# Joint steps for the first layer's sets 1 to 3, and the second layer's operands made from the sums

## The chip, the cores and the metric

The kernel runs on one core of a Trainium2 chip. The metric is device microseconds of one execution, the median of three runs. Lower is better.

## The reference

Attention with a forgetting decay, followed by two feed-forward layers, all in float32:

```python
scores = scale * q @ k.T ; scores = where(causal, -1e9, scores + decay)
x = softmax(scores) @ v                   # (4*576 tokens, 8*64 columns) = (2304, 512)
h = x @ w_in   ; x = (h - tanh(h)) @ w_out           # w_in (512, 2048), w_out (2048, 512)
h = x @ w_in2  ; x = (h * sigmoid(h)) @ w_out2       # the result
```

The weights arrive as float64; the kernel decodes them on the chip from their two 32-bit halves.

## The kernel before

**Numbers in two parts.** Each float32 matrix is split into a high part that TensorE takes without loss and a low remainder. A product is then three matmuls: high by high, high by low, low by high. The high part is a cast on ScalarE (ACT), the low part a subtraction on VectorE (DVE).

**Units.** The two layers are worked in 24 units: layer `l` (2), set `s` of 512 hidden columns (4, that is two weight chunks `q` of 256), token block `b` of 768 tokens (3). Units 0 to 11 are layer 1, units 12 to 23 layer 2. A product of two matrices cut 2 by 2 takes eight block products in the plain way; with sums and differences of blocks (Strassen's scheme) it takes seven. The seven operands of the token side are made once in a layer, written to DRAM (`xd`), and loaded again in each later unit.

**Slots.** Units below `U0` = 15 go through `slot_steps`, two slots a unit. A slot takes seven block products for `w_in` (`product`, L457; the first two units take eight, `plain`, L471). Each product lands in a PSUM bank, and DVE adds the products up one by one (L510). `bend` (L484) applies tanh or silu on ACT and, in layer 1, subtracts on DVE (L489). `high` and `low` split the result, and `project` (L427) takes eight block products for `w_out`, 96 matmuls of 384 columns a unit in layer 1; `gather` (L447) adds the sums to `x`. The operands of layer 2 are made in units 12 to 14 by `xtemp` (L324) and `xmake` (L337, L338, L342), a part of them on GpSimd (POOL).

**Joint steps.** Units 15 to 23 go through `joint`. There `h_step` (L634) and `c_step` (L675) take seven steps each for `w_in` and `w_out`, 12 or 18 matmuls a step, and add the products up inside PSUM. Between the steps ACT copies one running sum over another (L804, L870), so that fewer DVE additions are left. The steps of one unit's `w_out` alternate on TensorE with the next unit's `w_in`: h, c, h, c. `gate` (L797) applies the function, four times a unit; `two` (L807) makes the sums of the results, L839 and L840 split them, `gain` (L878) adds to `x`.

**What sets the order.** Every engine works through a fixed list. In the slots the list is written out by hand. In `joint` each piece of work is a `task` with an engine, a cost and a time at which it is meant to run, in steps of 2,080 ns; `planned` (L923) plays the list through and sorts it. TensorE's tasks keep their order; DVE and ACT take what is ready, at most three steps ahead of its time. The `keen` ones go first. The plan has no entry for a DMA.

**Weights.** `wjob` decodes a chunk: a scaling on ACT (L198), then shift, exponent, low, join on DVE (L202, L206, L209, L221), four sums of 256 columns (L225), and a split (L234 and L236 in the slots, L243 and L245 in `joint`). In the slots `w_out` needs no sums. There is one raw buffer for each of the two matrices; the load of the next chunk is issued after `low` (L160).

Of the kernel before, what the change touches and what calls it, by code (L numbers as in the profile page):

```python
# [37 lines left out]
U0 = 15  # L38
S0 = U0 // 3

# [4 lines left out]
def forgetting_attention_two_ffn(  # L45
# [106 lines left out]
    def wload(q, m, parts=(0, 1)):  # L152
# [17 lines left out]
        (((0, 4, 2),), ((8, 2, 6), (10, 1, 1))),  # L170
# [19 lines left out]
    def wjob(q, m, what, part=None):  # L190

        st = wjobs.setdefault((q, m), {})
        l, blocks = 2 * q // NFC, m == 0 or q >= 2 * S0
# [43 lines left out]
        else:  # L237
            for to, n, frm in GROUPS[m and l + 1][part]:
                hi, lo = (extra if to >= 8 else wtile)(q, m)
                to %= 8  # L240
                hi, lo, frm = hi[:, to:to + n], lo[:, to:to + n], st["s"][:, frm:frm + n]
# [350 lines left out]
    def ftile(u, what):  # L592
        k = u % 2
        if what == "12":
            if "12" not in small_tiles:
                small_tiles["12"] = pools["xb"].tile([P, 2, 2, TH], F32, tag="xo7", name="f_12")
            return small_tiles["12"][:, k]
        if what == "21":
            return flat(f"21_{k}", "hp", f"h{k}")
        if what == "1":  # L600
            return flat("1", "tp", "t0")
        if what == "22":
            return flat("22", "tp", "t1")
        return flat(what, "xt", {"a": "xt1", "b": "xt2"}[what])
# [4 lines left out]
    def ring_load(n):  # L609
# [4 lines left out]
        pool, tag = RING[n % 3]  # L614
        ring[u, i] = t = pools[pool].tile([P, 2, 2, TH], F32R, tag=tag, name=f"xr{n}")
        nc.sync.dma_start(out=rd(t).rearrange("p r k t -> p (r k t)"), in_=xd[l, b, i])
# [38 lines left out]
    def csteps(u):  # L655
        return STEPS if u < LASTU else (1, 5, 6, 2, 7, 3, 4)

    def c_step(u, k):
        l, i = units[u][0], csteps(u)[k]
        acc, fresh = cbank(u, i)  # L660
        t = gtile(7 * u + k)
        at = WAT[l][i]
        ws = [[w[:, at % 8] for w in (extra if at >= 8 else wtile)(2 * (u // NB) + j, 1)] for j in range(2)]
        for d in range(3 if l else 2):
            ds = slice(d * P, d * P + P)
            for j, (wh, wl) in enumerate(ws):
# [7 lines left out]
                for r, (w, m) in enumerate(terms):  # L674
# [3 lines left out]
                    )  # L678

# [24 lines left out]
    def joint():  # L704
        tasks, steps = [], 14
        tt_, copy = nc.vector.tensor_tensor, nc.scalar.copy

        def task(when, eng, cost, fn, reads=(), writes=(), keen=False):
            tasks.append((when, eng, cost, fn, reads, writes, keen))
# [7 lines left out]
        W2, N2 = dve(TB), act(TB)  # L717
        base = {u: steps * (u - U0) for u in range(U0, len(units) + 1)}
# [3 lines left out]


        def decode(q, m, when):
            l = 2 * q // NFC
            st = wjobs.setdefault((q, m), {})
            job, raw = (lambda *a: lambda: wjob(q, m, *a)), ("raw", m)

            def low():
                fill((q, m, "low"))  # L730

            yield "A", act(DM * 2), job("scale"), (raw,), (raw,)
            yield "V", 0.33, job("shift"), (raw,), ("wa",)
            yield "V", 0.33, job("exponent"), ("wa",), ("wb",)
            yield "V", dve(1024), low, (raw,), ("wb", raw)
            yield "V", dve(1024), job("join"), ("wa", "wb"), tuple(("ws", k) for k in range(4))
            for k, (to, p, op, r) in enumerate(RECIPE[m and l]):
                yield "V", dve(256), job("sum", k), (("ws", p), ("ws", r)), (("ws", to),)
            for g in range(2):
                cols = [("ws", k) for to, n, f in GROUPS[m and l + 1][g] for k in range(f, f + n)]  # L740
                n = 256 * len(cols)
                yield "A", act(n), job("HI", g), cols, (wkey(q, m, g),)
                yield "V", dve(n), job("LO", g), cols + [wkey(q, m, g)], (wkey(q, m, g),)

        def spread(t0, t1, parts):

            parts = [p if isinstance(p[0], float) or isinstance(p[0], int) else (None,) + p for p in parts]
            total = sum(c for _, e, c, *_ in parts if e == "V")
            t = t0
            for at, e, c, fn, r, w in parts:  # L750
                if at is not None:
                    t = max(t, at)
                task(t, e, c, fn, r, w)
                if e == "V":
                    t += (t1 - t0) * c / total

        for g in range(S0, 2 * NSET):
            t = base[3 * g]
            e, o = 2 * g + 2, 2 * g + 3
            if g == S0:  # L760
                a, b = list(decode(e - 2, 1, 0)), list(decode(o - 2, 1, 0))
                at = [(t + 2, a[-2]), (t + 10.5, b[-4]), (t + 14, b[-2])]
                parts = a + b
                t0, t1 = t, t + 16
            else:
                a, b = list(decode(o - 2, 0, 0))[-2:], list(decode(o - 2, 1, 0))
                at = [(t + 8.5, b[-4]), (t + 14.5, b[-2])]
                parts = a + b
                t0, t1 = t - 1, t + 15
            spread(t0, t1, [((next((w for w, p in at if p is j)),) if any(p is j for _, p in at) else ()) + j for j in parts])  # L770
            if e < 2 * NPR:
                a, b, c = list(decode(e, 0, 0)), list(decode(e, 1, 0)), list(decode(o, 0, 0))[:-2]
                at = t + 36.2
                parts = a + b + c
                spread(t + 16, t + 40, [((at,) if j is c[-2] else ()) + j for j in parts])


        for u in range(U0, len(units) + 1):
            t0 = base[u]
            if u < len(units):  # L780
# [13 lines left out]
                def gate(when, to, frm, kt, kf, tmp=None):  # L794
# [21 lines left out]
                gate(t0 + 11.55, g22, g22, f22, f22)  # L816
                gate(t0 + 12.0, g12, g12, f12, f12)
                if l:
# [8 lines left out]
                two(t0 + 15.3, g21, g21, tb, MINUS, f21, f21, fb, False)  # L827
# [5 lines left out]
                when[1], when[2] = 14.0, 14.5  # L833
                if u == LASTU:
                    when = dict(enumerate((10, 13.3, 13.4, 14.6, 15.6, 16.6, 17.6)))
                for k, i in enumerate(order):
                    n = 7 * u + k
                    g, (frm, kf), kg = gtile(n), src[i], n % 3
                    task(t0 + when[k], "A", N2, lambda g=g, f=frm: copy(g[:, 0], f), (kf,), (("gh", kg),))  # L839
                    task(t0 + when[k] + 0.1, "V", W2, lambda g=g, f=frm: tt_(g[:, 1], f, rd(g[:, 0]), MINUS),  # L840
                         (kf, ("gh", kg)), (("gl", kg),))
            v = u - 1
            if v < U0:
                task(t0 + 0.1, "A", 0, lambda: rest())
                for k in range(-1, 7):
# [561 lines left out]
```

## Time and profile before

| | before |
|---|---|
| median of three runs | 923.53 us (923.47 to 923.53) |
| the profiled execution's own time | 923.4 us |
| its span, first to last instruction | 921.4 us |
| TensorE busy, matmuls | 911.8 us (99%), 6006 |
| DVE busy | 764.8 us (83%) |
| ACT busy | 505.2 us (55%) |
| POOL busy | 174.0 us (19%) |
| granted TensorE clock, mean | 0.999 |

The profile is of one execution. Its span is 2.0 us shorter than that execution's time. Attention fills about the first 165 us; the slots run from there to about 634 us and the joint steps from 634 us to the end. A busy matmul is pipelined: its listed duration overlaps that of the next one, so the cost of one is read from start to start. The same holds, to a lesser degree, for DVE.

### The profile page before, as it was taken

What the parts mean: (1) busy time and instruction counts of PE and PEld (TensorE: products, weight loads), DVE (VectorE), ACT (ScalarE), POOL (GpSimd) and SP (SyncE); (2) the same over time, 40 slices, a digit from 0 to 9 for tenths busy, and PEclk for the clock granted to TensorE, in tenths of its full rate; (3) what the DMA queues carried; (4) which work ended last, traced back from release to release, by engine and by line L of the source; (5) the groups of instructions that cost most, each with busy time, mean ns of one, the idle gap of its engine ahead of it and who ended that gap; (6) DMA issues with size and microseconds to landing.
All of it is one profiled execution on the core that took longest, in us unless ns stands there. A gap on an engine that the chain in (4) does not pass through costs nothing.

```text
span 921.4 us, 15985 instructions
## 1 busy us (share of the span) xinstructions
PE 911.8 (99%) x6006; PEld 857.4 (93%) x6006; DVE 764.8 (83%) x1326; ACT 505.2 (55%) x871; POOL 174.0 (19%) x248
## 2 busy tenths in 40 slices
PE   8999999999999999999999999999999999999997
PEld 6777777799999999999999999899899999999997
DVE  7799998889878887888789898886779988977647
ACT  6888888666444332324242445564666666655443
POOL 8999999300000000000000010110000000000000
PEclk9999999999999999999999999999999999999999
DMA  5424442567548554855585456565677657655653
GB/s 166 150 97 159 160 139 84 220 249 298 222 199 331 208 206 158 331 180 220 172 304 190 169 206 217 186 232 210 244 247 255 233 199 269 200 178 200 210 184 121
DMA packets 48125, 188.94 MB, mean 205 GB/s; under 512 B 9456, under 2 KB 14064, under 8 KB 48016
## 3 DMA queue, kind: packets, MB, share of 16 engines
q1 hardware_dynamic: 47768, 187.64, 57.3%
q8 instruction: 47, 0.77, 0.3%
q10 hardware_dynamic: 280, 0.28, 0.1%
q14 instruction: 30, 0.25, 0.1%
HBM read 148.44 MB, written 38.34 MB: 203 GB/s over the span
## 4 chain that ended last, share of the span: by engine, by line
PE 95%; DVE 2%; ACT 1%; issue 1%; POOL 0%; DMA 0%; DVEq 0%; POOLq 0%
PE a L427 26%; PE h L457 20%; PE a L675 14%; PE h L634 14%; PE t L1139 5%; PE s L1092 5%; PE out_t L1195 4%; PE h L471 3%; PE s L1084 2%; PE h L675 0%; PE out L1195 0%; PE out_t L1223 0%; ACT gh L496 0%; POOL p L1127 0%; DMA de<-x 0%
## 5 line engine op out<-in xcount | busy, mean ns | idle before, releaser
L457 PE MATMUL h<-xo,wh 128*128 128x384 f32 x728 | 185.0, 334 | 0.0
L457 PEld LDWEIGHTS h<-xo,wh 128*128 128x128 f32 x728 | 132.0, 188 | 2.6
L634 PE MATMUL h<-xr,wh 128*128 128x384 f32 x504 | 128.5, 335 | 0.3 <-ACT h L804 0.3
L427 PE MATMUL a<-gh,wh 128*128 128x384 f32 x384 | 128.4, 334 | 0.0
L427 PE MATMUL a<-gl,wh 128*128 128x384 f32 x384 | 128.3, 334 | 0.0
L427 PE MATMUL a<-gh,wl 128*128 128x384 f32 x384 | 128.3, 334 | 0.0
L487 ACT ACTIVATE t<-hs 128x768 f32<-128x768 f32 x52 | 44.0, 847 | 145.9 <-DVE hs L510 145.9
L510 DVE TENSOR_TENSOR hs<-h,hs 128x384 f32<-128x384 f32 x182 | 100.6, 553 | 26.7 <-PE h L457 23.8
L457 PE MATMUL h<-xo,wl 128*128 128x384 f32 x364 | 121.8, 335 | 0.0
L634 PEld LDWEIGHTS h<-xr,wh 128*128 128x128 f32 x504 | 88.5, 189 | 1.4 <-ACT h L804 0.7
L338 POOL TENSOR_TENSOR xo<-xt,xo 128x768 fp32r<-128x768 f32 x3 | 6.2, 2071 | 425.8 <-ACT xo L337 425.8
L634 PE MATMUL h<-xr,wl 128*128 128x384 f32 x252 | 84.4, 335 | 0.0
L675 PE MATMUL a<-wh,gr 128*128 128x256 f32 x420 | 80.7, 282 | 0.0
L1113 ACT ACTIVATE p<-p,mn 128x128 f32<-128x128 f32 (+3 forms) x128 | 71.2, 558 | 16.9 <-DVE mn L1105 14.2
L1127 POOL TENSOR_SCALAR p<-p,sm 128x128 f32<-128x128 f32 (+3 forms) x128 | 72.7, 584 | 7.4 <-DVE sm L1124 6.9
L427 PEld LDWEIGHTS a<-gh,wh 128*128 128x128 f32 x384 | 72.1, 188 | 0.3 <-DVE x L447 0.3
L427 PEld LDWEIGHTS a<-gl,wh 128*128 128x128 f32 x384 | 72.1, 188 | 0.0
L427 PEld LDWEIGHTS a<-gh,wl 128*128 128x128 f32 x384 | 72.1, 188 | 0.0
L1105 DVE CUSTOM_DVE_ANT_0 p<-s,mask 128x128 f32<-128x128 f32 (+3 forms) x128 | 59.6, 479 | 14.3 <-PE s L1092 14.2
L500 DVE TENSOR_TENSOR gl<-t,gh 128x768 fp32r<-128x768 f32 x60 | 57.1, 952 | 14.1 <-ACT gh L496 13.9
L496 ACT CAST gh<-t 128x768 fp32r<-128x768 f32 x60 | 50.3, 839 | 32.8 <-DVE t L489 27.9
L457 PEld LDWEIGHTS h<-xo,wl 128*128 128x128 f32 x364 | 68.3, 188 | 0.0
(143 smaller groups left out, 2084.6 us busy)
## 6 DMA issues: line engine op xcount, KB each, us to landing
xo<-xd SPq DMA_DIRECT2D x63, 768.0 KB
xr<-xd SPq DMA_DIRECT2D x63, 768.0 KB
xd<-xo SPq DMA_DIRECT2D x42, 768.0 KB
raw<-w_in SPq DMA_DIRECT2D x32, 512.0 KB
raw<-w_out SPq DMA_DIRECT2D x32, 512.0 KB
kqraw<-kq SPq DMA_DIRECT2D x16, 608.0 KB
vraw<-v SPq DMA_DIRECT2D x16, 320.0 KB
out<-x SPq DMA_DIRECT2D x11, 384.0 KB
```

The costliest lines, as they stand in the source:

```text
L427: nc.tensor.matmul(dst, w, m, start=first and r == 0, stop=last and r == 2)
L457: nc.tensor.matmul(dst, w[:, ks], m[:, k], start=k == 0 and r == 0, stop=k == 1 and r == 2)
L496: nc.scalar.copy(gh, hs[h])
L500: nc.vector.tensor_tensor(gl, hs[h], rd(gh), ALU.subtract)
L510: nc.vector.tensor_tensor(to, p, s, ALU.add)
L634: nc.tensor.matmul(dst[:, j, 0:TH], w[:, ds], m[:, d], start=i in (1, 5) and d == r == 0, stop=d == 1 and r == 2, skip_group_check=True,)
L675: nc.tensor.matmul(dst, w, m, start=fresh and (l == 0 or d != 1) and j == r == 0, stop=j == 1 and r == 2, skip_group_check=True,)
L1092: nc.tensor.matmul(s[:, h, c:c + n], a[half(h), q], b[half(h), 0:n], start=r == 0, stop=r == 3,)
L1105: nc.vector.tensor_tensor_reduce(out=pt.rearrange("p (g c) -> p g c", g=2) if i == 4 else pt, in0=src, in1=m, op0=ALU.add, op1=ALU.min, sc ...
L1113: nc.scalar.activation(pt, pt, AF.Exp, bias=mn, scale=-1.0, accum_out=sums[:, n // 3 % 5, n % 3, 0:1],)
L1127: nc.gpsimd.tensor_scalar(pt, pt, sm[:, j:j + 1], 1.0, ALU.mult, ALU.mult)
L1139: nc.tensor.transpose(t[:, k], pt[:, c * P:c * P + P], ident)
```

## The change

`U0` goes from 15 to 3: units 3 to 14 leave the slots and enter `joint`. Units 3 to 11 (layer 1, sets 1 to 3) take seven steps for `w_in` and seven for `w_out`. Units 12 to 14 (layer 2, set 0), named `PLAIN`, take seven steps for `w_in` and eight block products for `w_out` (`plain_c`), whose sums ACT copies to `x`.

The operands of layer 2 are made by tasks in `joint` (`make`): four sums on DVE for each token block, in place in `x` (one of them in a spare tile, `tmp`), then seven splits (a cast on ACT, a subtraction on DVE) into the ring of three operand tiles from which `h_step` reads. Each is then written to DRAM by a DMA on SyncE's queue (`spill`). In the slots before, two of each unit's subtractions stood on POOL. The ring is loaded from DRAM for all other units.

In layer 1 a gate is a tanh on ACT and a subtraction on DVE; two of the four write the tanh to `tmp`. `planned` may now take a task up to eight steps ahead of its time (`EARLY`), and picks by a due time, the planned time plus a `spare`. Units 12 to 14 are planned one step longer. What was left of unit 2's work (`rest` and the first two of its remaining `project` calls) is issued ahead of the plan. The chunks of set 4 (layer 2, set 0) need no sums for `w_out`.

```diff
-U0 = 15
+U0 = 3
 S0 = U0 // 3
+PLAIN = (12, 13, 14)
+PLAINSETS = {u // NB for u in PLAIN if u >= NB * NSET}
...
-        l, blocks = 2 * q // NFC, m == 0 or q >= 2 * S0
+        l, blocks = 2 * q // NFC, m == 0 or q >= 2 * S0 and q // 2 not in PLAINSETS
...
+    def spill(n):
+        u, i = U0 + n // 7, STEPS[n % 7]
+        l, s, b = units[u]
+        d = xd[l, b, i] = dram.tile([P, 4 * TH], F32, name=f"xd{l}_{b}_{i}")
+        nc.sync.dma_start(out=d, in_=rd(ring[u, i]).rearrange("p r k t -> p (r k t)"))
...
+    def plain_c(u, c, a, t):
+        l, s, b = units[u]
+        acc, i = csums(u)[a], c // 10 - 1
+        fresh, last = i == 0 and s == 0, i == 1
+        for d in range(2 - a if l else 2):
+            for j in range(2):
+                q = 2 * (u // NB) + j
+                gh, gl = (t[:, e, j] for e in range(2))
+                if l:
+                    ds = slice((2 * a + d) * P, (2 * a + d) * P + P)
+                    wh, wl = (w[:, 2 * i:2 * i + 2].rearrange("p k f -> p (k f)") for w in wtile(q, 1))
+                    dst, terms = acc[:, d], ((gh[:, ds], wh), (gh[:, ds], wl), (gl[:, ds], wh))
...
     def joint():
-        tasks, steps = [], 14
+        rest()
+        for n in range(2):
+            project(16 * (U0 - 1) + n, False)
+        tasks = []
...
+            base[u + 1] = base[u] + 14 + (u - 1 in PLAIN)
...
+            if g == S0:
+                late = list(decode(o - 1, 1)) + late
+                spread(t, t + 15, late, at(o - 1, 1, 1, t + 2) | at(o, 1, 0, t + 10.5) | at(o, 1, 1, t + 11))
...
+        def make(u):
+            b, t0 = units[u][2], base[u]
...
+            def total(when, to, p, r, op=MINUS):
+                task(t0 + when, "V", W2, lambda: tt_(q[to](), q[p](), q[r](), op), (key[p], key[r]), (key[to],), False, 2)
+            total(-3.9, "11", "12", "11")
+            if less:
+                total(-3.5, "12", "22", "12", PLUS)
+                total(-1.5, "t", "12", "11")
...
+            total(0, "21", "21", "t")
...
+                kr, when = ("xr", n % 3), t0 + 2 * k - 4.6
+                def low(n=n, f=f):
+                    t = ring_tile(n)
+                    tt_(t[:, 1], q[f](), rd(t[:, 0]), MINUS)
+                    spill(n)
+                task(when, "A", N2, lambda n=n, f=f: copy(ring_tile(n)[:, 0], q[f]()), (key[f],), (kr,), False, 2)
+                task(when + 0.1, "V", W2, low, (key[f], kr), (kr,), False, 2)
...
-                    r = [kd] + [wkey(q + j, 0, k // 4) for j in range(2)]
+                    r = [kd, ("xr", (7 * (u - U0) + k) % 3)] + [wkey(q + j, 0, k // 4) for j in range(2)]
...
-                    t, k = (tmp, "tmp") if tmp is not None else (to, kt)
-                    task(when, "A", N2, lambda f=func: nc.scalar.activation(t, frm, f), (kf,), (k,), True)
-                    task(when + 0.45, "V", W2, lambda: tt_(to, frm, t, MINUS), (kf, k), (kt,), True)
+                    t, k = (lambda: ftile(0, "tmp"), "tmp") if tmp else (lambda: to, kt)
+                    task(when, "A", N2, lambda f=func: nc.scalar.activation(t(), frm, f), (kf,), (k,), True)
+                    task(when + 0.45, "V", W2, lambda: tt_(to, frm, t(), MINUS), (kf, k), (kt,), True)
...
-        LAG = 0.1
+        LAG, EARLY = 0.1, 8
...
-                return max([end[d] + LAG * (tasks[d][1] != e) for d in deps[n]] + [tasks[n][0] - 3])
+                return max([end[d] + LAG * (tasks[d][1] != e) for d in deps[n]] + [tasks[n][0] - EARLY])
```

## Rows read from the trace of the kernel before

**Rows 1.** The page's first part: busy us (share of the span), instructions.

```profile
PE 911.8 (99%) x6006; PEld 857.4 (93%) x6006; DVE 764.8 (83%) x1326; ACT 505.2 (55%) x871; POOL 174.0 (19%) x248
```

**Rows 2.** Busy us of each engine in stretches of the span.

```profile
core 0: us, PE busy (x) PEld busy (x) DVE busy (x) ACT busy (x) POOL busy (x), PEclk, DMA share, GB/s
240.00:500.00 260.00, 260.00 (x1502) 260.00 (x1501) 216.58 (x302) 97.18 (x121) 0.00 (x0) 1.00 0.61 225
630.00:680.00 50.00, 49.69 (x282) 46.16 (x281) 37.83 (x49) 30.02 (x38) 0.00 (x0) 1.00 0.64 223
680.00:710.00 30.00, 30.00 (x214) 29.73 (x213) 28.83 (x36) 19.55 (x25) 0.00 (x0) 1.00 0.65 221
770.00:800.00 30.00, 30.00 (x214) 29.91 (x214) 29.21 (x38) 18.29 (x23) 0.00 (x0) 1.00 0.65 221
680.00:800.00 120.00, 120.00 (x851) 119.45 (x850) 108.21 (x138) 74.47 (x94) 0.00 (x0) 1.00 0.68 230
```

**Rows 3.** Timeline of TensorE, joint steps: start us, us, then the instruction.

```profile
713.75 0.28 PE L675 MATMUL a<-weh,gr 128*128 128x256 f32 x1
713.87 0.28 PE L675 MATMUL a<-wel,gr 128*128 128x256 f32 x1
...
715.18 0.34 PE L634 MATMUL h<-xr,wl 128*128 128x384 f32 x1
715.35 0.51 PE L634 MATMUL h<-xr,wh 128*128 128x384 f32 x2
```

**Rows 4.** Timeline of DVE in the joint steps, back to back.

```profile
700.40 0.95 DVE L886 TENSOR_TENSOR x<-x 128x768 f32<-128x768 f32 x1
701.27 0.95 DVE L840 TENSOR_TENSOR gr<-f,gr 128x768 fp32r<-128x768 f32 x1
702.14 1.22 DVE L245 TENSOR_TENSOR wl<-ws,wh 128x1024 fp32r<-128x1024 f32 x1
703.28 0.95 DVE L878 TENSOR_TENSOR x<-a,x 128x768 f32<-128x768 f32 x1
...
706.60 0.70 DVE L206 TENSOR_SCALAR wb<-wa 128x1024 uint32<-128x1024 uint32 x1
707.33 1.22 DVE L209 SCALAR_TENSOR_TENSOR wb<-raw,wb 128x1024 f32<-128x1024 uint32 x1
...
710.59 0.42 DVE L225 TENSOR_TENSOR ws<-ws 128x256 f32<-128x256 f32 x1
710.93 0.95 DVE L878 TENSOR_TENSOR x<-a,x 128x768 f32<-128x768 f32 x1
...
720.50 0.68 DVE L202 TENSOR_SCALAR wa<-raw 128x1024 uint32<-128x1024 uint32 x1
721.10 0.95 DVE L807 TENSOR_TENSOR f_a<-f,f 128x768 f32<-128x768 f32 x1
```

**Rows 5.** DVE timeline, then TensorE timeline: one split, and the step that reads it.

```profile
696.33 0.95 DVE L840 TENSOR_TENSOR gr<-f,gr 128x768 fp32r<-128x768 f32 x1
...
699.98 0.28 PE L675 MATMUL a<-wh,gr 128*128 128x256 f32 x1
```

**Rows 6.** Timelines of SyncE's queue and of ACT, start of the joint steps.

```profile
640.24 0.81 SPq L160 DMA_DIRECT2D raw<-w_out  x2
...
645.05 1.14 ACT L198 ACTIVATE raw<-raw 128x1024 f32<-128x1024 f32 x1
```

**Rows 7.** POOL's groups from 500 to 660 us: busy us, mean ns.

```profile
L338 POOL TENSOR_TENSOR xo<-x,xo 128x768 fp32r<-128x768 f32 x3 | 6.7, 2236 | 0.0
L338 POOL TENSOR_TENSOR xo<-xt,xo 128x768 fp32r<-128x768 f32 x3 | 6.2, 2071 | 425.8 <-ACT xo L337 425.8
```

**Rows 8.** Waits of SyncE's queue: total us, times, longest us.

```profile
SPq L342 <- DVE xo L338: 115.9, 29, 14.7
```

More of the change, by code (lines that the diff above doesn't have):

```diff
@@ L715, in act, with decode @@
             return (n / 0.96 + 60) / 2080
-        W2, N2 = dve(TB), act(TB)
-        base = {u: steps * (u - U0) for u in range(U0, len(units) + 1)}
+        W2, N2, basis = dve(TB), act(TB), {}
+        base = {U0: 0}
+        for u in range(U0, len(units)):
+            base[u + 1] = base[u] + 14 + (u - 1 in PLAIN)
         def wkey(q, m, k):
             return "w", q % NSLOT, m, k
-        def decode(q, m, when):
+        def decode(q, m):
             l = 2 * q // NFC
[L726 to L736, printed above, removed]
-            for k, (to, p, op, r) in enumerate(RECIPE[m and l]):
[L738 to L743, printed above, removed]
@@ L745, in spread @@
-        def spread(t0, t1, parts):
-            parts = [p if isinstance(p[0], float) or isinstance(p[0], int) else (None,) + p for p in parts]
-            total = sum(c for _, e, c, *_ in parts if e == "V")
+            job, raw = (lambda *a: lambda: fill((q, m) + a)), ("raw", m)
+            yield "A", act(DM * 2), job("scale"), (raw,), (raw,), None
+            yield "V", 0.33, job("shift"), (raw,), ("wa",), None
+            yield "V", 0.33, job("exponent"), ("wa",), ("wb",), None
+            yield "V", dve(1024), job("low"), (raw,), ("wb", raw), None
@@ new lines, in decode @@
+            if m and q // 2 in PLAINSETS:
+                key = wkey(q, 1, 0)
+                yield "V", dve(1024), job("join"), ("wa", "wb"), ("wa",), None
+                yield "A", act(1024), job("hi"), ("wa",), (key,), 0
+                yield "V", dve(1024), job("lo"), ("wa", key), (key,), None
+                return
+            yield "V", dve(1024), job("join"), ("wa", "wb"), tuple(("ws", k) for k in range(8)), None
+            for k, (to, p, op, r) in enumerate(RECIPE[m and l]):
+                yield "V", dve(256), job("sum", k), (("ws", p), ("ws", r)), (("ws", to),), None
@@ new lines, in decode, with spread @@
+            groups = [0, 1, 2] if m and q // 2 in MIXED else [0, 1]
+            for g in groups[::-1] if m and q % 2 and 3 * (q // 2) - 1 in PLAIN else groups:
+                cols, key = [("ws", k) for to, n, f in GROUPS[m and l + 1][g] for k in range(f, f + n)], wkey(q, m, g)
+                yield "A", act(256 * len(cols)), job("HI", g), cols, (key,), g
+                yield "V", dve(256 * len(cols)), job("LO", g), cols + [key], (key,), None
+        def spread(t0, t1, jobs, since):
+            total = sum(c for e, c, *_ in jobs if e == "V")
@@ L759, in joint @@
-            e, o = 2 * g + 2, 2 * g + 3
+            t, t2 = base[3 * g], base[3 * g + 3]
+            o = 2 * g + 1
+            late = list(decode(o, 1))
             if g == S0:
[L761 to L764, printed above, removed]
-            else:
[L766 to L775, printed above, removed]
+                late = list(decode(o - 1, 1)) + late
+                spread(t, t + 15, late, at(o - 1, 1, 1, t + 2) | at(o, 1, 0, t + 10.5) | at(o, 1, 1, t + 11))
+            elif 3 * g - 1 in PLAIN:
+                spread(t - 1, t + 15, list(decode(o, 0))[-2:] + late, at(o, 1, 0, t + 15))
+            else:
+                spread(t - 1, t + 15, list(decode(o, 0))[-2:] + late, at(o, 1, 0, t + 8.5) | at(o, 1, 1, t + 14.5))
@@ L923, in planned @@
     def planned(tasks):
-        LAG = 0.1
+        LAG, EARLY = 0.1, 8
         tasks = sorted(tasks, key=lambda t: t[0])
         writer, readers, deps = {}, {}, []
-        for n, (when, eng, cost, fn, reads, writes, keen) in enumerate(tasks):
+        for n, (when, eng, cost, fn, reads, writes, keen, due) in enumerate(tasks):
             d = {writer[k] for k in reads if k in writer}
@@ L955, in planned @@
                 now = [n for r, n in known if r <= t]
-                n = min(now, key=lambda n: tasks[n][0])
-                if not tasks[n][6] and tasks[n][0] > t - 2:
+                n = min(now, key=lambda n: tasks[n][7])
+                if not tasks[n][6] and tasks[n][7] > t - 2:
                     soon = [r for r, k in known if tasks[k][6] and t < r < t + tasks[n][2] - 0.2]
```

147 lines of the change are left out of this document (115 added, 32 removed).

## The prediction

> **What bounds the kernel now.** I read the page's first part, then the stretches, then single instructions in the timelines. TensorE is busy for 99% of the span and DVE for 83% [rows 1]. A busy share alone proves little for an engine that pipelines, so the stretches come next. In layer 1's slots, 240 to 500 us, TensorE is busy for all of 260 us with 1502 matmuls of 384 columns [rows 2]: 260 / 1502 = 0.173 us from one to the next. The joint steps, 680 to 800 us, show no idle time either, and their matmuls follow each other at 0.17 us for 384 columns and 0.12 us for 256 [rows 3]. So TensorE sets the time; what is taken from it comes off the end, as long as no other engine takes its place. The next in line is DVE: 108.21 of 120 us in the joint steps [rows 2]. ACT, with 74.47 of 120 us there, is far off.
>
> **What is removed.** A unit of layer 1 has 84 matmuls for `w_in` and 96 for `w_out` in the slots, and 84 and 84 in joint steps. Nine units (3 to 11) lose 12 each: 108 matmuls, each 0.173 us, **18.7 us**. A unit goes from 180 x 0.173 = 31.1 us to 168 x 0.173 = 29.1 us. Units 12 to 14 gain nothing: eight block products before and after, 72 matmuls of 512 columns each. So the page should count 6006 - 108 = 5898. The floor is 923.4 (the profiled execution's own time) - 18.7 = 904.7 us; the median of the runs lies 0.1 us above that execution, so 904.8 us.
>
> One rule bears on the size of this term. The Trainium skill ("TensorE: Matmul & The Clock Gate", section "Wait — 56ns, not 53.3ns?") gives back-to-back matmuls N / 2.4 GHz plus about 2.5 ns, an estimate of 162.5 ns for 384 columns and 17.6 us for 108 of them. The trace has 173 ns for these float32 matmuls, and the measurement decides; the sum keeps 18.7 us.
>
> **What is added on DVE in layer 1.** This is where the gain can go. I count a joint unit of layer 1 in instructions of 768 columns: two sums of the running products, four tanh subtractions (layer 2 has none, its gates are ACT's alone), four sums of the results, seven low parts, five additions to `x`: 22, against 18 for a joint unit of layer 2. Back to back one takes 0.87 us from start to start (700.40, 701.27, 702.14) [rows 4]. Over the nine units that is 9 x 22 = 198, plus three changes of basis, plus six instructions of `make` that are planned before unit 12 begins, less twelve that end behind that point (low parts, last sums and additions of unit 11, of which some replace unit 2's): 195 x 0.87 = 170 us. A weight chunk takes 0.60 + 0.73 + 1.14 + 1.14 + 4 x 0.34 + 1.14 + 0.60 + 0.34 = 7.05 us: shift, exponent, low, join, four sums, split [rows 4]; the split's part of 512 columns has no row there and is put at the shift's 0.60, a choice. Eleven whole chunks fall into the nine units, one without sums (4.7 us) and one nearly whole (6.1 us): 88 us. Together **258 us** of DVE, beside 9 x 29.1 = 262 us of TensorE: 98%.
>
> So the bound of the cost runs from 0 to this: in the joint steps of layer 2 DVE shows as busy for 108.21 / 120 x 29.6 = 26.7 us a unit (84 matmuls at 0.173 and 126 at 0.12 make a unit of 29.6 us); four more at their listed 0.95 us give 30.5 us a unit, 1.4 us above TensorE, 12.6 us over nine units. The listed durations overlap when DVE is packed, so I hold to the count. How full can DVE be while TensorE does not wait? The two densest stretches of 30 us have it at 28.83 and 29.21 us, 96 and 97%, with TensorE at 30.00 [rows 2]. 258 us packed at 97% need 266 us, 4 us over 262. The third set is worst: the chunks of set 4 and `make` come on top there. I take **5 us** of waiting on TensorE, between 0 and 12.6 us.
>
> **The chain behind the gate.** In layer 1 a gate's result is later by one DVE subtraction, 0.87 us. The tightest place is the second `c_step` of a unit. In layer 2 its low part ended at 697.28 us and the step began at 699.98 us, 2.7 us later [rows 5]. With the subtraction 1.8 us are left, so alone it costs nothing; with a filled queue on DVE it is part of the 5 us. Behind a late low part stand all of TensorE's steps.
>
> **The move of layer 2's operands.** `make` issues 11 instructions of 0.87 us on DVE for each of units 12 to 14, 21 in all of them the low parts. Before, 6 of these 21 stood on POOL at over 2 us each [rows 7]; so DVE has some 6 x 0.87 = 5 us more. Cover: those units need no products added on DVE, no combined results and no additions to `x` (ACT copies); 17 instructions and some 8 us of weights make 23 us beside a unit of 31 us. Without that cover the price would be the 5 us. The 21 writes to DRAM move from the slots into SyncE's queue of the plan; the count and bytes are the same. In that queue a write waits for DVE's low part, up to 14.7 us before [rows 8], and behind it stand the weight loads, planned many steps ahead, while the ring's own loads are not needed there. Nothing is added for it. The first `h_step` of layer 2 now waits for an operand that DVE has just made; its data are a unit old, and it is late only if DVE is. This is in the 5 us.
>
> **Looser order.** With eight steps instead of three, ACT's scaling of a chunk can be placed right behind the freeing of the raw buffer, and the plan knows nothing of the load between. The nearest row: load issued at 640.24 us, scaling begun at 645.05 us [rows 6], so at most 4.8 us. The worst place is unit 3, where two `w_out` chunks follow each other. ACT would stand still for up to 4.8 us, with 1 to 3 us of room before the next copy of a sum: 0 to 3 us once. I take 0, since the third step there has its slack, and keep 3 in the range. The seam of slots and joint steps cost 0.31 us at 630 to 680 us [rows 2]; it moves to unit 2 and keeps its price. In the last nine units the looser order can gain nothing, TensorE being full, and DVE's idle tenth covers a loss.
>
> **Sum.** 923.4 - 18.7 + 5 = 909.7 us, and 0.1 for the median: **909.8 us**.
>
> **Rivals.**
> *DVE keeps up.* The free tasks fill every gap and unit 3, which has less of `x` to add, takes work ahead. For it: 97% is already reached without a wait. Against: 98% would have to hold for nine units. 904.8 us, within 904.5 and 906.5. Chance 0.22.
> *DVE is the new bound.* The busy share, not the count, is right: 904.8 + 12.6 = 917.4 us; 915.5 to 921.7. Against: the overlap of listed durations in rows 4. Chance 0.16.
> *Slower: the gate's chain in every unit.* DVE's list is fixed, and 1.8 us are left before the second `c_step`. If five other instructions (4.35 us) stand ahead of the low part, TensorE waits 2.5 us in each of nine units, 22.7 us, and the time is 904.8 + 22.7 = 927.5 us. It decides at 1.8 + 2.07 = 3.9 us of work ahead, four or five instructions, since a unit saves 2.07 us. For it: DVE is nearly full. Against: the gates are keen and go first. Chance 0.07.
> *The change doesn't do what it says.* If the nine units still issue 96 matmuls for `w_out`, the time stays at 923.5 us. The diff shows seven steps of 12; chance 0.05.
>
> **How the numbers follow.** The forecast, 906.5 to 915.5 us, has 0.50. The range of 904.5 to 920 us leaves out the slower case, the unchanged one and the upper end of the bound by DVE, some 0.15, and a little below. A measurement of this kernel can tell about 0.2%, 1.8 us: faster, below 921.7 us, 0.50 + 0.22 + 0.15 = 0.87; within, 0.06; slower 0.07.
>
> **What would show it.** 5898 matmuls; nine units of 29 to 30 us where 31.1 stood; DVE above 95% busy between units 3 and 12, and TensorE's idle time there some 5 us, ended by DVE or by ACT behind DVE, most of it near the end of layer 1; POOL idle after attention. Wrong would be: TensorE's gaps ended by a copy on ACT behind a scaling (the looser order), by an operand or weight load (SyncE's queue), or by DVE in every unit.

## The result, and the profile after

The changed kernel takes 930.09 us (median; 927.47 to 930.49) against 923.52 us before: a ratio of 1.0065, with a 95% interval of 1.0047 to 1.0084. It is slower by 6.6 us where 909.8 us was forecast, and it lies above the range of 904.5 to 920 us.

| | before | after |
|---|---|---|
| the profiled execution's own time | 923.4 us | 930.35 us |
| its span | 921.4 us | 927.7 us |
| matmuls | 6006 | 5898 |
| DVE busy | 764.8 us | 785.2 us |
| granted TensorE clock, mean | 0.999 | 0.993 |

The page's first part for the kernel after, as in [rows 1]:

```profile
PE 902.3 (97%) x5898; PEld 844.6 (91%) x5898; DVE 785.2 (85%) x1307; ACT 575.6 (62%) x969; POOL 161.2 (17%) x242
```

The 108 matmuls are gone, and TensorE's busy share still fell from 99% to 97%. Busy time of a pipelined engine says little about how much it waited, so I worked that out from the starts: the time from each matmul's start to the next one's, less the usual one (0.1735 us for 384 columns, 0.12 for 256, 0.23 for 512, as the kernel before has them), summed from 185 us on. Call it TensorE's lost time. It was 1.5 us before and is 26.7 us after. So -18.7 + 25.2 = +6.5 us, nearly the whole of the 6.95 us between the two profiled executions. The gain was made in full, and more than given back.

The stretches show where (columns as in [rows 2]; kernel after):

```profile
240.00:280.00 40.00, 35.12 (x193) 34.48 (x192) 31.18 (x44) 18.76 (x24) 0.00 (x0) 0.96 0.48 177
480.00:520.00 40.00, 39.77 (x230) 39.45 (x229) 39.38 (x49) 26.99 (x35) 0.00 (x0) 1.00 0.64 223
520.00:560.00 40.00, 36.67 (x197) 36.36 (x196) 38.94 (x49) 24.97 (x32) 0.00 (x0) 0.91 0.43 168
300.00:540.00 240.00, 235.48 (x1335) 232.56 (x1336) 227.15 (x284) 143.36 (x186) 0.00 (x0) 0.99 0.62 219
```

The holes are at both ends of the nine units: 193 and 197 matmuls in 40 us, where 230 fit at full pace (the row of 480 to 520 us). The lost time by place: about 11.6 us in unit 3 (1.5 at its first `h_step`, 5.4 at a load, 4.7 at copies of unit 2's sums), 7.0 us in units 4 to 11, 6.1 us before unit 12, and 1.7 us at 671 us, where a weight's cast and low part are late. The 1.5 us of the first `h_step`, which waits for its copy on ACT, stand in every kernel below, whatever its edit. What ended TensorE's waits from 190 us on (engine line, releaser: total us, times, longest us):

```profile
PE h L654 <- ACT h L906: 11.1, 6, 3.7
PE a L706 <- ACT x L447: 2.9, 1, 2.9
PE a L706 <- DVE gr L950: 1.1, 1, 1.1
```

The largest releaser is ACT, and not one of its long works: L906 is the copy of one running sum over another that a step of `h_step` starts from. ACT is busy for 62% of the span. Why it was late is read at three places.

**Unit 3, the load.** ACT's timeline there, and SyncE's queue (kernel after):

```profile
266.30 0.81 SPq L163 DMA_DIRECT2D raw<-w_out  x2
...
263.41 0.80 ACT L906 COPY h<-h 128x768 f32<-128x768 f32 x1
271.31 1.11 ACT L201 ACTIVATE raw<-raw 128x1024 f32<-128x1024 f32 x1 [7.10 <-DMA raw<-w_out]
272.32 0.91 ACT L245 CAST weh<-ws 128x512 fp32r<-128x512 f32 x2
273.14 0.80 ACT L902 ACTIVATE f<-h 128x768 f32<-128x768 f32 x1
273.84 1.03 ACT L245 CAST wh<-ws 128x1024 fp32r<-128x1024 f32 x1
274.99 0.83 ACT L949 CAST gr<-f 128x768 fp32r<-128x768 f32 x1
275.73 0.79 ACT L906 COPY h<-h 128x768 f32<-128x768 f32 x1
```

ACT reached the scaling (L201) at 264.21 us, 2.1 us before the load was even issued, and stood 7.1 us. Five instructions followed ahead of the copy, and TensorE waited for it:

```profile
276.57 1.01 PE L654 MATMUL h<-xr,wh 128*128 128x384 f32 x2 [3.70 <-ACT h L906]
277.38 0.52 PE L654 MATMUL h<-xr,wl 128*128 128x384 f32 x1
277.70 0.52 PE L654 MATMUL h<-xr,wh 128*128 128x384 f32 x1
```

Behind that wait the matmuls follow each other at 0.32 us instead of 0.173 us. The two stretches around it give the clock:

```profile
272.00:276.00 4.00, 0.87 (x5) 0.55 (x4) 3.54 (x6) 3.89 (x7) 0.00 (x0) 1.00 0.65 232
276.00:280.00 4.00, 3.43 (x11) 3.43 (x12) 3.97 (x5) 1.94 (x3) 0.00 (x0) 0.57 0.23 66
```

The mean granted clock from 276 to 280 us is 0.57: most of it at the lower of the two levels (1.2 GHz), behind 4 us in which TensorE was busy for 0.87 us. Ten matmuls run about 0.146 us late each before 2.4 GHz is back. In the whole kernel about 5.7 of the 26.7 us are of this kind, behind three waits (at 276, 300 and 547 us).

**Unit 3, the copies of unit 2.** ACT again, 25 us later (kernel after):

```profile
296.88 0.83 ACT L949 CAST gr<-f_b 128x768 fp32r<-128x768 f32 x1 [3.21 <-DVE f_b L909]
297.62 0.79 ACT L447 COPY x<-a 128x768 f32<-128x768 f32 x1
298.31 0.80 ACT L906 COPY h<-h 128x768 f32<-128x768 f32 x1
```

The copy of unit 2's sum (L447) frees the PSUM bank that a step of `c_step` needs. It stands behind a cast that waits 3.2 us for a sum of DVE (`f_b`). With the low clock behind it this costs 4.7 us.

**Units 4 to 11.** DVE's sum, the cast and copy on ACT, the matmul (kernel after):

```profile
331.10 0.95 DVE L909 TENSOR_TENSOR f_b<-f,f_a 128x768 f32<-128x768 f32 x1
...
332.14 0.83 ACT L949 CAST gr<-f_b 128x768 fp32r<-128x768 f32 x1 [3.70 <-DVE f_b L909]
333.01 0.78 ACT L906 COPY h<-h 128x768 f32<-128x768 f32 x1
...
333.85 0.62 PE L654 MATMUL h<-xr,wh 128*128 128x384 f32 x2 [0.91 <-ACT h L906]
```

The pattern is the same: DVE is late with `f_b`, ACT waits 3.70 us with its cast, and the copy that TensorE needs, whose own data are there (the last `h_step` gave way to a `c_step` at 330.69 us), stands behind that cast. It comes back at 423 and 454 us with 1.1 to 1.2 us each, and before unit 12, at 543.53 us, with 3.49 us and the low clock after it.

### The profile page after: what moved, and what is told of

The parts are those of the page before. It is cut to its first block, busy times and chain, and to the rows that moved or that the text cites. A ratio compares the mean times of both kernels' runs of the same rounds, so it can differ in the third digit from the quotient of the medians.

```text
span 927.7 us, 15808 instructions
## 1 busy us (share of the span) xinstructions
PE 902.3 (97%) x5898; PEld 844.6 (91%) x5898; DVE 785.2 (85%) x1307; ACT 575.6 (62%) x969; POOL 161.2 (17%) x242
## 4 chain that ended last, share of the span: by engine, by line
PE 55%; DVE 12%; ACT 2%; issue 1%; DVEq 0%; ACTq 0%
PE h L654 26%; PE a L706 23%; PE a L742 5%; DVE f L903 2%; DVE f L909 2%; DVE gr L950 2%; DVE x L993 1%; DVE f_a L909 1%; DVE f_b L909 1%; DVE wl L247 1%; ACT a L985 1%; PE h L706 0%; PE a L429 0%; ACT f_tmp L902 0%; DVE ws L224 0%
## 5 line engine op out<-in xcount | busy, mean ns | idle before, releaser
L654 PE MATMUL h<-xr,wh 128*128 128x384 f32 x1176 | 302.1, 338 | 11.1 <-ACT h L906 11.1
L654 PEld LDWEIGHTS h<-xr,wh 128*128 128x128 f32 x1176 | 211.8, 190 | 14.8 <-ACT h L906 13.0
L654 PE MATMUL h<-xr,wl 128*128 128x384 f32 x588 | 198.1, 337 | 0.0
L654 PEld LDWEIGHTS h<-xr,wl 128*128 128x128 f32 x588 | 111.4, 189 | 0.0
L950 DVE TENSOR_TENSOR gr<-f,gr 128x768 fp32r<-128x768 f32 x102 | 97.0, 951 | 11.9 <-ACT gr L949 11.8
L949 ACT CAST gr<-f 128x768 fp32r<-128x768 f32 x102 | 85.2, 836 | 30.2 <-PE a L706 28.0
L993 DVE TENSOR_TENSOR x<-a,x 128x768 f32<-128x768 f32 (+1 forms) x73 | 67.7, 930 | 17.2 <-PE a L706 17.0
L706 PE MATMUL a<-gr,wh 128*128 128x384 f32 x288 | 76.4, 344 | 4.5 <-ACT x L447 2.9
L1238 DVE CUSTOM_DVE_ANT_0 p<-s,mask 128x128 f32<-128x128 f32 (+3 forms) x128 | 59.6, 479 | 14.3 <-PE s L1225 14.3
L706 PEld LDWEIGHTS a<-wh,gr 128*128 128x128 f32 x420 | 67.5, 190 | 0.5 <-ACT wh L245 0.5
L706 PE MATMUL a<-weh,gr 128*128 128x256 f32 x312 | 60.3, 283 | 0.0
L906 ACT COPY f<-h 128x768 f32<-128x768 f32 x42 | 33.6, 801 | 34.5 <-PE h L654 24.5
L906 ACT COPY h<-h 128x768 f32<-128x768 f32 x42 | 33.0, 785 | 26.6 <-PE h L654 26.4
```

What stands on the lines that cost most here:

```text
L654: nc.tensor.matmul(dst[:, j, 0:TH], w[:, ds], m[:, d], start=i in (1, 5) and d == r == 0, stop=d == 1 and r == 2, skip_group_check=True,)
L706: nc.tensor.matmul(dst, w, m, start=fresh and (l == 0 or d != 1) and j == r == 0, stop=j == 1 and r == 2, skip_group_check=True,)
L906: task(when, "A", N2, lambda: copy(to, frm), (kf,), (kt,), True)
L949: task(w, "A", N2, lambda g=g, f=frm: copy(g[:, 0], f), (kf,), (("gh", kg),), False, 2)
L950: task(w + 0.1, "V", W2, lambda g=g, f=frm: tt_(g[:, 1], f, rd(g[:, 0]), MINUS), (kf, ("gh", kg)), (("gl", kg),), False, 2)
L993: task(when, "V", n, lambda: tt_(to, *((frm, to) if op == PLUS else (to, frm)), op), (kf, kx[c]), (kx[c],), True)
```

## The experiments

All edits are against the changed kernel. "Lost time" is TensorE's, worked out as above for each kernel's profiled execution.

**e1: the load of a raw chunk gets an entry in the plan.**

```diff
             yield "V", dve(1024), job("low"), (raw,), ("wb", raw), None
+            yield "S", 2.5, lambda: None, (), (raw,), None
```

> The plan gets an entry of 2.5 steps (5.2 us) for the load of a raw weight chunk, between the freeing of its buffer and the next scaling. Theory A (ACT's fixed list stands behind a load that the plan does not know): the 7.1 us in which ACT waited for w_out at the seam go, TensorE gets back about 6.9 us between 262 and 280 us, and the time is 923 to 925 us. Theory B (DVE is the bound, whatever stands first on ACT): the wait comes back as one on DVE within unit 3, 928 to 931 us.

Measured: 924.2 us (922.0 to 926.1), 5.9 us less than the kernel after; ratio to before 1.0007 (0.9996 to 1.0018). Lost time 19.0 us. ACT's timeline at the same place:

```profile
271.53 0.84 ACT L950 CAST gr<-f 128x768 fp32r<-128x768 f32 x1
272.27 1.16 ACT L201 ACTIVATE raw<-raw 128x1024 f32<-128x1024 f32 x1
273.32 0.82 ACT L907 COPY h<-h 128x768 f32<-128x768 f32 x1
```

Casts that stood behind the scaling now stand ahead of it, and the scaling waits for nothing. The wait of 3.87 us at the seam is 0.99 us. The one behind unit 2's copies, 3.08 us, is still there, as its own cause would have it. Theory A's range holds the time: the load was a cause by itself.

Its own price is less than the whole gain. From 266 to 294 us the lost time falls from 5.4 to 1.1 us, so 4.3 us are the load's. Most of the rest of the fall from 26.7 to 19.0 us is clock: two waits that the edit doesn't touch are as long as in the kernel after, and here the granted clock stays up behind them. The one before unit 12, 3.49 us in both kernels, e1 first (before and behind the wait), then the kernel after (behind it):

```profile
538.00:542.00 4.00, 0.68 (x5) 0.36 (x4) 4.00 (x5) 2.44 (x4) 0.00 (x0) 1.00 0.13 51
542.00:546.00 4.00, 3.65 (x19) 3.24 (x20) 3.96 (x7) 3.69 (x5) 0.00 (x0) 1.00 0.00 0
...
547.00:553.00 6.00, 5.81 (x19) 5.81 (x20) 5.97 (x9) 3.83 (x6) 0.00 (x0) 0.52 0.04 16
```

The ten executions of e1 differ in the same way: five of 922.0 to 923.4 us have a mean granted clock of 0.997 to 0.999, five of 925.0 to 926.1 us one of 0.993 to 0.996, with one list of instructions. So some 3 us of these times go with the clock, and differences of that size between two kernels need the clock beside them.

**e2: unit 2's copies are planned on the engine that does them.**

```diff
-                        task(t0 + 2 * k + 2.05, "V", W2, lambda m=m: gather(m), (kg,), (kg,), True)
+                        task(t0 + 2 * k + 2.05, "A", N2, lambda m=m: gather(m), (kg,), (kg,), True)
```

> Unit 2's four copies of sums to x are planned on ACT, where they run, and not on DVE. Theory A (they stand on ACT behind a cast that waits for DVE, because the plan does not see them there): the gap of 3.1 us at 296.7 us and the slow clock behind it go, 4.9 us, time 925 us. Theory B (they are late only because the load of the chunk delayed all of unit 3): no change within 1 us, 929 to 931 us.

Measured: 930.72 us (929.7 to 931.3), ratio 1.0077 (1.0062 to 1.0092). The wait at 296 us has gone, and a new one of 5.6 us stands at 443 us. The plan is one list, so a change of one entry moves what follows. The gain was real where it was meant and was lost elsewhere; neither theory foresaw that. The time lies in Theory B's range (929 to 931), but B's reason falls: the wait went although the load still held up unit 3 (3.67 us there).

**e3: three steps ahead instead of eight.**

```diff
-        LAG, EARLY = 0.1, 8
+        LAG, EARLY = 0.1, 3
```

> A task may run three steps ahead of its time, as before, and not eight. Theory A (the looser order brought the wait for the load): the wait at the seam shrinks to under 2 us, 5 us are gained there, but DVE has less to choose from and some of it is lost again in units 4 to 11: 924 to 929 us. Theory B (DVE's load alone decides, and the looser order was its remedy): worse than 930, 931 to 940 us.

Measured: 931.65 us (930.7 to 932.3), ratio 1.0088 (1.0073 to 1.0103). The wait at the load fell from 3.87 to 0.28 us, so the looser order did cause it; but TensorE now waits 3.98 us at 353.8 us, for this cast of a weight (ACT's timeline):

```profile
356.13 0.83 ACT L949 CAST gr<-f_b 128x768 fp32r<-128x768 f32 x1 [2.96 <-DVE f_b L909]
356.87 1.04 ACT L245 CAST wh<-ws 128x1024 fp32r<-128x1024 f32 x1
```

It is the same head of the line, `gr<-f_b`, with something else behind it. The time lies above what Theory A gave (924 to 929): its mechanism was there, and its gain went to another place. Theory B's range (931 to 940) holds it. In lost time three steps gain 5.0 us at the load (5.4 to 0.4 us) and lose 9 us in units 4 to 11 (7 to 16 us). So the looser order cost TensorE a wait at the load, and by these medians it was worth 1.6 us in all.

**e4: the tanh is not subtracted.** In units 3 to 11 the gate is a plain tanh on ACT, as layer 2's gates are. This takes four DVE subtractions from each of those units and shortens the gate's chain by one instruction.

```diff
-                    if l:
+                    if True:
                         task(when, "A", N2, lambda f=func: nc.scalar.activation(to, frm, f), (kf,), (kt,), True)
                         return
```

> The subtraction of tanh from h is left out in units 3 to 11, so a unit has 18 DVE instructions of 768 columns there instead of 22. Theory A (a full DVE makes TensorE wait): the 7.1 us of gaps in units 4 to 11 and the 6.3 us before unit 12 go, unit 3's 11.8 us stay, time 915 to 918 us. Theory B (the waits come from loads and from ACT's order alone): 927 us or more.

Measured: 917.62 us (916.9 to 919.6), ratio 0.9934 (0.9917 to 0.995). From 300 to 540 us:

```profile
300.00:540.00 240.00, 237.81 (x1372) 237.39 (x1371) 210.66 (x265) 152.02 (x195) 0.00 (x0) 1.00 0.65 226
```

1372 matmuls stand where the kernel after has 1335. DVE's busy time there fell from 227 to 211 us, and between 300 and 530 us no matmul is left that came over 0.2 us late. Theory A's range (915 to 918) holds the median, though not by A's own sum. Unit 3 lost 6.6 us where A kept all it had lost, since the copies of unit 2's sums no longer wait (nothing is lost from 294 to 310 us): that wait too came from a late gate. And 5.6 us were lost from 650 to 680 us, at a weight's cast and low part and a low clock behind them.

**e5: e1 and e2 together.**

> Both corrections of the plan together: the load of a raw chunk has an entry of 2.5 steps, and unit 2's copies to x are planned on ACT. Theory A (the seam's loss is these two): of the 11.8 us lost in unit 3 about 10 us come back, the waits for DVE in units 4 to 11 and before unit 12 stay, 919 to 922 us. Theory B (the list is so full that a gap closed at one place opens at another): 924 to 929 us.

Measured: 925.87 us (925.5 to 926.9), ratio 1.0029 (1.0018 to 1.004). The seam's three waits are 1.35, 0.97 and 0.58 us. But the new wait of e2 is here too (timelines of ACT and TensorE):

```profile
442.88 0.83 ACT L950 CAST gr<-f_b 128x768 fp32r<-128x768 f32 x1 [1.95 <-DVE f_b L910]
443.61 1.04 ACT L245 CAST wh<-ws 128x1024 fp32r<-128x1024 f32 x1
...
444.71 1.01 PE L654 MATMUL h<-xr,wh 128*128 128x384 f32 x2 [5.42 <-ACT wh L245]
```

So with the seam mended, 22.9 us are still lost, as Theory B had it (924 to 929). Theory A (919 to 922) falls.

**e6: e5, with the low parts of the weights and of `make` on POOL.** In the plan POOL is a fifth engine. This kernel doesn't compute the whole reference, and why is not settled (e12, with the half in `make` alone, does), so its time stands for its list of instructions only.

```diff
-                    nc.vector.tensor_tensor(lo, frm, rd(hi), ALU.subtract)
+                    nc.gpsimd.tensor_tensor(lo, frm, rd(hi), ALU.subtract)
...
-                yield "V", dve(256 * len(cols)), job("LO", g), cols + [key], (key,), None
+                yield "G", gp(256 * len(cols)), job("LO", g), cols + [key], (key,), None
...
-                    tt_(t[:, 1], q[f](), rd(t[:, 0]), MINUS)
+                    nc.gpsimd.tensor_tensor(t[:, 1], q[f](), rd(t[:, 0]), MINUS)
...
-                task(when + 0.1, "V", W2, low, (key[f], kr), (kr,), False, 2)
+                task(when + 0.1, "G", gp(TB), low, (key[f], kr), (kr,), False, 2)
```

> Both corrections, and the low parts of the weight chunks and of layer 2's operands move from DVE to POOL, which is idle after attention: 2.1 us of DVE a chunk and 6.1 us a unit of 12 to 14. Theory A (a full DVE is what makes TensorE wait in units 4 to 11 and before unit 12): DVE falls to about 90%, most of the 13 us of waits go, 907 to 912 us. Theory B (it is the fixed order on ACT, whatever DVE's load): within 3 us of the run with both corrections alone.

Measured: 954.46 us (953.2 to 955.0), ratio 1.0334 (1.0319 to 1.0349). DVE has 87 instructions fewer than in the kernel after and is no less busy. One group of it (busy us, mean ns) and one instruction, with POOL's beside it:

```profile
L954 DVE TENSOR_TENSOR gr<-f,gr 128x768 fp32r<-128x768 f32 x32 | 38.8, 1219 | 0.0
...
392.57 3.01 DVE L954 TENSOR_TENSOR gr<-f,gr 128x768 fp32r<-128x768 f32 x1
...
392.40 2.37 POOL L247 TENSOR_TENSOR wl<-ws,wh 128x1024 fp32r<-128x1024 f32 x1 [5.89 <-ACT wh L245]
```

A split that takes 0.95 us alone takes 3.01 us beside a POOL subtraction. The time lies outside both theories' ranges: A wanted 907 to 912 us, B a time within 3 us of e5.

**e7: joint steps from unit 9 only.** Units 3 to 8 stay in the slots. In this kernel one `w_out` chunk (6) is scaled twice, so it doesn't compute the reference: one more scaling (36 where the others have 35) and a repeated split are issued.

```diff
-U0 = 3
+U0 = 9
```

> The joint steps begin at unit 9 instead of 3, nothing else is changed: six of the nine units stay in the slots, 72 of the 108 matmuls saved are back. Theory A (each seam and the passage to layer 2 have a price of their own, and a middle unit of layer 1 gains 2.07 us less about 0.8 us of waits): 6.2 us are gained, 6 to 7 us are lost at the seam for the load and 6.3 us before unit 12: 928 to 932 us. Theory B (the middle units lose as much as they save): 924 to 927 us, as the seam without the misplaced copies is the only loss.

Measured: 934.95 us (934.6 to 935.4), ratio 1.0125 (1.0108 to 1.0142), with 5970 matmuls. Three units save 36 x 0.173 = 6.2 us, and 19.7 us are lost: 923.5 - 6.2 + 18.2 = 935.5. So the loss shrinks far less than the number of units (26.7 us for nine); entry into the joint steps and the passage to layer 2 carry most of it (waits of 3.79 us at 459.8, 2.85 us at 483.9 and 2.63 us at 551.3 us). The scaling twice may have a part in this that I can't separate. Theory B (924 to 927) falls; A had the direction and not the size (928 to 932).

**e8: e5, with each DVE instruction 62 ns dearer in the plan.** The plan then orders by nearer the listed durations; nothing else changes.

```diff
-            return (n / 0.96 + 68) / 2080
+            return (n / 0.96 + 130) / 2080
```

> Both corrections, and the plan is told a DVE instruction costs 65 ns more than now, so that it sees DVE late where it is late; the work is the same. Theory A (TensorE waits since ACT's list puts a cast that waits for DVE ahead of the copy or the weight's cast that TensorE waits for): the plan puts them in the other order, 2 to 5 us better than with both corrections alone, 915 to 919 us. Theory B (DVE's work itself is too much, in any order): the same within 2 us, or worse.

Measured: 928.07 us (926.5 to 928.8), ratio 1.0048 (1.0033 to 1.0063). The waits move to 349.7 us (3.2), 443.9 us (3.5 and 1.7) and 540 us (3.4). Theory A (915 to 919) falls and Theory B holds: a plan with dearer DVE costs doesn't by itself order better.

**e9 and e10: e5, with one unit of each set of layer 1 taking eight block products for `w_out`.** The third of a set in e9, the first in e10. Each such unit has twelve matmuls more and a lighter DVE. Both kernels also plan a part of unit 3's `w_out` weights later: the last split of its first chunk and all of its second one, at 14.3 to 15.9 steps into the unit instead of spread over its first 15. So they can be compared with each other, and only roughly with e5. These kernels don't compute the whole reference, and why is not settled; their times too stand for their lists of instructions only.

```diff
-PLAIN = (12, 13, 14)
+PLAIN = (5, 8, 11, 12, 13, 14)      # e9;  e10: (3, 6, 9, 12, 13, 14)
...
-                late = list(decode(o - 1, 1)) + late
-                spread(t, t + 15, late, at(o - 1, 1, 1, t + 2) | at(o, 1, 0, t + 10.5) | at(o, 1, 1, t + 11))
+                a = list(decode(o - 1, 1))
+                spread(t, t + 6, a[:-2], at(o - 1, 1, 1, t + 2))
+                spread(t + 14.3, t + 15.9, a[-2:] + late, {})
```

> Both corrections of the plan, and units 5, 8 and 11 (the third token block of each set of layer 1) take eight block products for w_out: 36 matmuls more, 6.2 us of the 18.7 us are given up, but such a unit has 10 DVE instructions of 768 columns instead of 22. Theory A (a full DVE makes TensorE wait): DVE falls to about 85% there, the waits of units 4 to 11 and before unit 12 shrink to some 3 us, 914 to 918 us, better than with seven everywhere. Theory B (the gaps come from the fixed lists, whatever DVE's load): 6 us slower than both corrections alone, 930 us or more.

> As the run with units 5, 8 and 11, with units 3, 6 and 9 (the first token block) instead. Theory A: DVE's relief now falls at the seam and at the start of each set, and not before unit 12, whose operands DVE makes: the 6.3 us there stay, 917 to 922 us. Theory B (the place doesn't matter): within 1.5 us of the run with 5, 8 and 11.

Measured: e9 929.92 us (928.7 to 930.9), ratio 1.0069 (1.0054 to 1.0084); e10 922.59 us (920.8 to 923.7), ratio 0.9988 (0.9978 to 0.9998). Both have 5934 matmuls. From 300 to 540 us, e9 first:

```profile
300.00:540.00 240.00, 232.17 (x1311) 228.33 (x1312) 205.72 (x262) 141.06 (x185) 0.00 (x0) 0.99 0.65 223
...
300.00:540.00 240.00, 236.97 (x1362) 235.55 (x1361) 208.17 (x264) 149.33 (x197) 0.00 (x0) 1.00 0.64 223
```

DVE's load is the same within 3 us, and the lost time in this stretch is 14.3 us against 4.1 us (19.8 and 13.2 us in the whole kernels). So how full DVE is doesn't by itself set the loss; the order of the instructions on it and on ACT does as much. In e9 most of TensorE's waits end with a weight's cast and low part, and not behind `f_b`:

```profile
PE a L706 <- ACT wh L245: 4.9, 4, 2.0
PE a L706 <- DVE wl L247: 4.0, 4, 1.5
```

e9 comes near Theory B (930 or more), and not by a gap behind the gate. e10 lies just above Theory A's 917 to 922, and far from Theory B's 1.5 us around e9.

**e11: e5 without the tanh subtraction** (left out as in e4).

> Both corrections of the plan, seven products in all nine units, and the subtraction of tanh from h left out in units 3 to 11 (18 DVE instructions a unit instead of 22). Theory A: with neither the seam's two losses nor a full DVE the saved matmuls come through but for some 3 to 5 us: 908 to 911 us. Theory B (something else holds the joint steps of layer 1): 915 us or more.

Measured: 913.46 us (911.2 to 914.7), ratio 0.9889 (0.9872 to 0.9906). The same stretch, e5 first, then e11:

```profile
300.00:540.00 240.00, 231.88 (x1319) 229.69 (x1317) 225.72 (x283) 139.77 (x180) 0.00 (x0) 0.99 0.63 219
...
300.00:540.00 240.00, 237.80 (x1373) 237.49 (x1372) 212.50 (x268) 151.40 (x193) 0.00 (x0) 1.00 0.66 228
```

Lost time 8.5 us in all, and between 300 and 525 us no matmul over 0.2 us late; 3.2 us stand before unit 12 and 2.9 us at 653 us. The same seven-step scheme, with DVE busy for 13 us less of the 240 and a gate's chain shorter by one instruction, runs at TensorE's pace in these units. The step from e5 to e11 is 925.87 - 913.46 = 12.4 us. Its time lies between the two theories (908 to 911, and 915 or more), nearer to A's mechanism.

**e12: e5, with only `make`'s 21 low parts on POOL.** The edit is the third and fourth pair of lines of e6.

> Both corrections of the plan, and of layer 2's operands the 21 low parts alone on POOL; the weights' low parts stay on DVE. Theory A (before unit 12 TensorE waits for a DVE that has make's instructions on top): three of them leave the stretch before unit 12, the 3.5 us there shrink by 2 us or more, and the time is 922 to 924 us. Theory B (an instruction on POOL slows DVE's two-input instructions beside it, as in the run with all low parts on POOL, where the mean of the 768-column split rose from 951 to 1219 ns): no gain, 925 to 929 us, with DVE's splits over 1.0 us where POOL is busy.

Measured: 935.82 us (934.9 to 936.4), ratio 1.0131 (1.0114 to 1.0148): 10 us slower than e5 and worse than even Theory B had it, lost time 32.3 us. POOL's timeline and DVE's at the passage to layer 2, then two groups from 530 to 615 us:

```profile
546.41 2.52 POOL L875 TENSOR_TENSOR xr<-f_tmp,xr 128x768 fp32r<-128x768 f32 x1 [3.49 <-ACT xr L878]
549.26 2.18 POOL L875 TENSOR_TENSOR xr<-x,xr 128x768 fp32r<-128x768 f32 x1 [0.32 <-ACT xr L878]
...
547.20 2.55 DVE L954 TENSOR_TENSOR gr<-f,gr 128x768 fp32r<-128x768 f32 x1
549.79 2.47 DVE L913 TENSOR_TENSOR f<-f,f_b 128x768 f32<-128x768 f32 x1
...
L875 POOL TENSOR_TENSOR xr<-x,xr 128x768 fp32r<-128x768 f32 x14 | 30.2, 2160 | 390.5 <-ACT xr L878 390.5
L954 DVE TENSOR_TENSOR gr<-f,gr 128x768 fp32r<-128x768 f32 x11 | 17.5, 1600 | 0.0
```

DVE's two instructions end 0.82 us after the POOL instructions beside them end (548.93 and 551.44 us). That is about one DVE instruction's own time, which fits instructions that did nothing until POOL was done. In e5 the same group has a mean of 951 ns. What DVE is spared it loses again in waiting. The first of the two rows is a late low part that TensorE waits for, 4.16 us at 545.5 us; another wait, 3.55 us at 587.6 us, ends with a copy on ACT behind a weight's cast that had waited 4.64 us for DVE's sums.

The Trainium skill ("SBUF — State Buffer", section "🔬 SBUF: two separate sides") has DVE instructions with two inputs in SBUF and GpSimd instructions that read SBUF lock the same ports for a whole instruction, the other standing still. These two rows agree.

None of the kernels that compute the whole reference beats the kernel before; e1 equals it.

## Why the prediction was wrong

**Right: what is removed.** 5898 matmuls, 108 fewer at 0.173 us. In e11 the median is 913.46 us with 8.5 us lost; the floor of 904.8 us plus 7 us more of lost time than before gives 911.8 us, against 911.2 us of the execution in which it was read.

**Wrong: "Looser order ... I take 0, since the third step there has its slack".** The wait for the load cost 5.4 us in the kernel after, and 4.3 us of them come back in e1 (the median gains 5.9 us, with the clock), where I kept "0 to 3 us once". In all, three steps instead of eight were no better (e3): the order had a gain in units 4 to 11 that I had also put at nothing. The load itself was as in [rows 6], 5.0 us from issue to the scaling (266.30 to 271.31). Two things were missed. The price of a wait runs from the moment the engine arrives, and ACT arrived 2.1 us before the load was issued: 7.1 us. And the slack I named was one instruction's; five stood between the scaling and the copy. The prediction listed this wait as the sign of being wrong, but gave it neither a price nor a chance that fitted.

**Wrong: the seam "keeps its price" of 0.31 us** [rows 2]. Unit 2's copies cost 4.7 us there, and the first `h_step` 1.5 us. I had read the seam of two units of layer 2 and moved the number to a seam of two units of layer 1, where the work beside it on ACT and DVE is another: the copies stood behind a gate's late result, and with the tanh subtraction left out (e4) their wait is gone.

**Mis-sized: 5 us for a full DVE.** The experiments give 12.4 us (e5 to e11, the low clock behind the waits included), at the upper bound of 12.6 us that I had kept but not taken; in the trace of after it is 7.0 us in units 4 to 11 and 6.1 us before unit 12. The step that failed is "how full can DVE be while TensorE does not wait?". I answered it from stretches of layer 2 [rows 2], at 96 and 97%. They still run so after the change (TensorE busy for all of 680 to 710 us with DVE at 29.04 of 30). But layer 1's gate is one DVE instruction longer, and its results are due at fixed places in ACT's list. The loss comes from single late instructions, not from the sum: 227 us busy in 240 us, and e9 and e10 lose 14.3 and 4.1 us from 300 to 540 us at nearly the same load.

**Not foreseen: the clock.** In the kernel after, each wait of 3 to 4 us was followed by a few us at half clock, about 5.7 us in all. I priced waits at their length alone. It isn't a fixed price either: in e1 two waits of the same length at the same places left the clock at 1.00.

**The rivals.** The sum of 927.5 us of the slower rival lies near the result, but its mechanism, 2.5 us at the second `c_step` of each of nine units, isn't what happened: in units 4 to 11 matmuls of a `c_step` that waited for a split lost about 2.7 us in all, 1.22 us the longest, and those of an `h_step` behind ACT 3.4 us. That rival did name a root, DVE's later gate; it looked at DVE's list alone, and more of the harm was done in ACT's. "DVE keeps up" and "the change doesn't do what it says" fall by the trace. As for "DVE is the new bound", its size was right for the DVE part, and its mechanism was not, as e9 and e10 show.

**What stays open.** Whether an order of these same instructions exists that loses only what e11 loses. Each plan tried here (e1, e2, e3, e5, e8) closed some waits and opened others. e4 and e11 take away a DVE load and a link of a chain together, so the share of each in the 12.4 us isn't told apart. Nor does a run show what decides whether the clock falls behind a wait of 3 to 4 us.

## What to carry to other kernels

When work is taken from the engine that sets the time, ask of each other engine what its list holds at each place, not only how full it is: here an engine that was 62% busy stopped TensorE most, mostly because a cast that waited for a late engine, or a scaling that waited for a load, stood ahead of a copy whose data were there. A plan that orders the engines' lists must hold the DMAs too, with the time from issue to landing. A price read at a seam holds for the work that stands beside it and has to be read anew where the seam moves.

## What the runs showed of the hardware that I had not expected

- A wait of 3 to 4 us on TensorE can cost more than its length, and need not. In the kernel after, 4 us with TensorE busy for 0.87 us were followed by 4 us with a mean granted clock of 0.57, in which matmuls of 384 columns came every 0.32 us. In e1, 4 us with TensorE busy for 0.68 us were followed by 4 us at 1.00. The Trainium skill ("TensorE: Matmul & The Clock Gate", section "Wait — 56ns, not 53.3ns?") gives N / 1.2 GHz for the cold clock, an estimate of 0.320 us for 384 columns; the trace agrees.
- A DVE subtraction of 768 columns beside one on POOL takes 2.5 to 3.0 us instead of 0.95 us; the mean of a group that is partly beside POOL goes from 951 to 1600 ns (e12).
